# How many zero matmuls TensorE gets in each step of a two-layer transformer kernel

## The chip, the cores and the metric

The kernel runs on one core of a Trainium2 chip. A core has TensorE (matrix products, called PE in a profile), ScalarE (ACT), VectorE (DVE), GpSimd (POOL) and the queue engine SyncE (SP). The metric is the time on the device, in microseconds, of one execution: the median of several runs.

## The reference

One sequence of S = 2048 tokens with D = 640 features goes through attention block A, token mixer B, A again and B again, with the same weights both times. A has 32 heads of 20 features, B has F = 1536 hidden rows and mixes over the tokens.

```python
def _A_ref(x, wqkv, wo):
    qkv = (x @ wqkv).reshape(B, S, 3, H, Dh).transpose(2, 0, 3, 1, 4)
    q, k, v = qkv[0], qkv[1], qkv[2]
    scores = jnp.einsum("bhqd,bhkd->bhqk", q, k) * (Dh ** -0.5)
    p = _softmax(scores, axis=-1)
    o = jnp.einsum("bhqk,bhkd->bhqd", p, v)
    return o.transpose(0, 2, 1, 3).reshape(B, S, D) @ wo

def _B_ref(x, w1, b1, w2, b2):
    h = _layernorm(x, axis=-1)
    u = _gelu(jnp.einsum("bsd,sf->bdf", h, w1) + b1)
    y = jnp.einsum("bdf,fs->bds", u, w2) + b2
    return y.transpose(0, 2, 1)

x = x + _A_ref(_layernorm(x), wqkv, wo)
x = x + _B_ref(_layernorm(x), w1, b1, w2, b2)
x = x + _A_ref(_layernorm(x), wqkv, wo)
x = x + _B_ref(_layernorm(x), w1, b1, w2, b2)
```

## The kernel before

The program has five parts: the set-up with the first layer norm and the projections to V (0 to 50 us), the first attention stage (to 937 us), the first token mixer with the second layer's projections (to 1052 us), the second attention stage (to 1937 us) and the second mixer. The change lies in `attention`, which is written out twice, once for each layer.

The work of a stage is cut into units (qb, g, kt): a block of 512 queries (four of them), a group of four heads (eight) and a tile of 128 keys (16). A unit has four chunks, one for each head, of 128 keys by 512 queries. For one chunk PE makes scores S (`s_matmul`, L441) into one bank of PSUM; the exponential of them is made either by ScalarE (L474) or, for some chunks of the last key tiles, by VectorE with a polynomial (L351, L368, L374, L381, L386); PE then multiplies it by V (`emit_PV`, L683) into the accumulator `acc` of the group. Four matmuls of one PV go to four column strips of the array and start together.

Chunks are packed into score tiles `S` of three banks. `tiles[t]` is a pair: the chunks that ScalarE takes in one exponential (three, or two when the third belongs to VectorE), and the VectorE chunk or None. A step t of the loop at the end of `attention` is one such exponential; a step with fewer than three ScalarE chunks is called short. There are 683 steps in each stage. The planner counts 1.344 us for a full step and 0.92 us for a short one. There are two `S` tiles, so the scores of step t+2 wait for the exponential of step t, and only one `acc`, so the first PV of a group waits until the last group's sum has been read.

The order of the work on PE is the order in which the loop writes it, and it is kept by a chain (`pe`). In step t this is: the scores of step t+1 (`emit_S`); the PVs whose exponentials are of step t-1 or earlier; zero matmuls (`keep_busy`); side work (`emit_fills`). ScalarE's exponential of step t is written between the first two. After the 16th PV of a group `normalize` puts four VectorE instructions into that engine's queue: a transpose that reads `acc` (L486), a reciprocal, a product and a second transpose (L493).

Side work is a queue of groups of matmuls: projections of later heads to K and Q (L240, five matmuls of 512 columns), the product with `wo` (L579, L614) and the first product of the mixer (L551), each with 512-column groups and 128-column groups. A step takes 1.5 units of it if it has a PV or is short, and 3.0 otherwise, until a group ends; the step after a group's end takes none (`FILL_GAP`). `planned_fill` says ahead of a step whether it will have side work (`has_fill`). VectorE copies a finished group out of the one `misc` bank (L557, L642, and others).

A zero matmul (L464) multiplies a block of zeros by a block of ones and adds the result to a bank that is in use, which leaves it as it was. One pass is four such matmuls of 512 columns, one for each column strip. The loop before the change writes `SLOTS - 1 - n_pv - short` passes (`SLOTS` is 4, `n_pv` the number of PVs of the step) in steps without side work and with an accumulator that is in use; none where side work is planned, and none between a group's last PV and the next group's first, where `acc_tiles` is empty.

## Time and profile before

| what | value |
|---|---|
| median of 3 runs | 2018.26 us (2015.72 to 2019.93) |
| the profiled execution's own time | 2025.45 us |
| its span, first to last instruction | 2023.7 us |
| mean granted clock of TensorE | 0.975 |
| PE busy | 1723.9 us, 85% |
| ACT busy | 1801.0 us, 89% |
| DVE busy | 1388.9 us, 69% |
| POOL busy | 155.1 us, 8% |
| exponentials of ScalarE | 1366, 1709.1 us |
| zero matmuls | 5232 rows |

In the profile a row names the source line, the engine, the operation, the tile that it writes and those that it reads, their shapes, the number of such instructions, the busy time in microseconds and the mean of one in nanoseconds; behind the second bar stands the engine's idle time just before these instructions, and what ended most of it ("<-PE S L441" is a PE instruction of line 441 that writes S). A matmul's row lasts some 0.17 us longer than its columns stream, because its end is modelled; matmuls in sequence overlap, and the distance of their starts tells their cost. `PEclk` is the granted clock in tenths of full speed. In a table by stretches, each engine's busy time is followed by the number of its instructions; then come the granted clock, the share of the DMA engines and the GB/s.

### The profile page before, as it was taken

To read this page: it belongs to the slowest core of one execution; us is meant where nothing else is said; L and a number is where in the kernel's file an instruction comes from. 1 tells how busy PE (TensorE), PEld (TensorE's weight loads), DVE (VectorE), ACT (ScalarE), POOL (GpSimd) and SP (SyncE) were. 2 spreads that over 40 slices of the span, in tenths; PEclk is the share of its full clock that TensorE was granted. 3 is DMA by queue.
4 is the path that set the end of the run, shared out by engine and by line. 5 is a ranking of instruction groups with operands and counts; after the bars stand their busy time and mean duration, and the time that the engine had idled before them with its cause. 6 is when DMAs were issued, how large, how long until landed. Compare 5 with 4: busy or idle time off the path is not lost.

```text
span 2023.7 us, 39147 instructions
## 1 busy us (share of the span) xinstructions
PE 1723.9 (85%) x16395; PEld 615.5 (30%) x16592; DVE 1388.9 (69%) x2091; ACT 1801.0 (89%) x1504; POOL 155.1 (8%) x220
## 2 busy tenths in 40 slices
PE   7888888888888887887998888888888888878879
PEld 4222222232222222223542222222222222222235
DVE  6777787666766577773557787777657765767742
ACT  5999999999999999996349999999999999999952
POOL 2000000110012001110000000001000220011000
PEclk9999999999999999998999999999999999999989
DMA  6000000110134012214620000112101430233145
GB/s 135 1 1 1 1 19 26 67 49 8 34 67 68 1 40 45 42 21 136 207 83 1 1 1 1 34 33 69 38 14 40 79 56 2 59 51 43 15 149 185
DMA packets 90768, 97.34 MB, mean 48 GB/s; under 512 B 9696, under 2 KB 68192, under 8 KB 90592
## 3 DMA queue, kind: packets, MB, share of 16 engines
q1 hardware_dynamic: 70464, 71.22, 11.3%
q0 software_dynamic: 20128, 23.62, 7.8%
q8 instruction: 129, 2.11, 0.4%
q14 instruction: 47, 0.39, 0.1%
HBM read 55.48 MB, written 39.32 MB: 47 GB/s over the span
## 4 chain that ended last, share of the span: by engine, by line
ACT 34%; PE 23%; DVE 22%; issue 19%; DMA 1%; POOL 0%; SPq 0%; another core or an unknown queue 0%; ACTq 0%; DVEq 0%; POOLq 0%
ACT P L474 34%; PE S L441 6%; PE y L897 5%; DVE ew L351 4%; PE acc L683 3%; DVE et L374 3%; DVE Pd L381 3%; PE acc L464 2%; DVE ey L368 2%; DVE Pd L386 2%; PE pp L231 2%; DVE T L486 1%; PE misc L551 1%; PE misc L240 1%; DVE T L491 1%
## 5 line engine op out<-in xcount | busy, mean ns | idle before, releaser
L474 ACT ACTIVATE P<-S 128x1536 bf16<-128x1536 f32 (+1 forms) x1366 | 1709.1, 1447 | 58.5 <-PE S L441 43.9
L441 PE MATMUL S<-QTq,KT 32*128 32x512 bf16 x4096 | 574.6, 388 | 198.9 <-ACT P L474 137.9
L683 PE MATMUL acc<-P,Vaug 128*32 128x512 bf16 x3764 | 388.9, 396 | 27.3 <-DVE T L486 26.6
L351 DVE TENSOR_SCALAR ew<-S 128x512 int32<-128x512 f32 x332 | 226.1, 681 | 262.6 <-PE S L441 262.3
L441 PEld LDWEIGHTS <-KT 32*128 32x128 bf16 x4096 | 195.9, 91 | 689.0 <-issue 539.0
L464 PE MATMUL acc<-zr,zw 128*32 128x512 bf16 x5232 | 404.4, 388 | 0.0
L374 DVE SCALAR_TENSOR_TENSOR et<-ey 128x1024 f32<-128x1024 f32 x166 | 202.5, 1220 | 4.4
L386 DVE SCALAR_TENSOR_TENSOR Pd<-ew,Pd 128x1024 int16<-128x1024 int16 x166 | 201.3, 1213 | 2.4
L381 DVE SCALAR_TENSOR_TENSOR Pd<-et,ey 128x1024 bf16<-128x1024 f32 x166 | 200.6, 1208 | 1.6
L683 PEld LDWEIGHTS <-Vaug 128*32 128x32 bf16 x4096 | 108.1, 93 | 278.3 <-issue 278.1
L464 PEld LDWEIGHTS <-zw 128*32 128x32 bf16 x5232 | 128.8, 97 | 97.2 <-issue 41.0
L557 DVE COPY ustg<-misc 128x512 f32<-128x512 f32 (+1 forms) x144 | 69.4, 482 | 109.1 <-PE misc L551 89.6
L182 POOL TENSOR_TENSOR rstd<-veps,mhalf 128x1 f32<-128x1 f32 x64 | 38.9, 608 | 1168.9 <-DVE veps L177 1049.7
L562 POOL DMA_DIRECT2D uacc<-ustg x96 | 86.2, 899 | 435.0 <-DVE ustg L557 421.6
L368 DVE TENSOR_SCALAR ey<-ew 128x1024 f32<-128x1024 uint16 x166 | 114.8, 692 | 2.9
L551 PE MATMUL misc<-h2st,w1st 128*128 128x128 bf16 (+1 forms) x512 | 104.7, 300 | 6.6 <-DVE ustg L557 5.3
L897 PE MATMUL y<-uT,w2s 128*128 128x128 bf16 (+1 forms) x754 | 106.8, 298 | 3.8 <-ACT uT L840 3.1
L240 PE MATMUL misc<-hh,wq_pad 128*128 128x512 bf16 x268 | 84.9, 384 | 6.2 <-DVE KT L642 2.5
L240 PE MATMUL misc<-hh,wk_pad 128*128 128x512 bf16 x250 | 78.6, 388 | 6.9 <-DVE KT L642 5.0
L486 DVE STREAM_TRANSPOSE T<-acc 128x512 f32<-128x512 f32 x64 | 45.5, 711 | 55.5 <-PE acc L683 55.5
L579 PE MATMUL misc<-wo_pad,attnT 128*128 128x128 bf16 (+1 forms) x362 | 73.6, 303 | 2.0 <-issue 1.0
L897 PEld LDWEIGHTS <-w2s 128*128 128x128 bf16 x768 | 59.7, 98 | 49.4 <-issue 4.6
(86 smaller groups left out, 898.8 us busy)
## 6 DMA issues: line engine op xcount, KB each, us to landing
uacc<-ustg POOLq DMA_DIRECT2D x72, 256.0 KB, 4.0
w2s<-in_B_w_dram SPq DMA_DIRECT2D x16, 768.0 KB
w1st<-in_B_w_dram SPq DMA_DIRECT2D x36, 256.0 KB
x1in<-xd SPq DMA_DIRECT2D x24, 320.0 KB
ua<-uacc SPq DMA_DIRECT2D x24, 320.0 KB
xd<-x2s SPq DMA_DIRECT2D x16, 320.0 KB
xin<-xd SPq DMA_DIRECT2D x16, 320.0 KB
uacc<-ustg POOLq DMA_DIRECT2D x72, 64.0 KB, 2.8
```

Of the source, the lines that this page charges most:

```text
L240: pe(nc.tensor.matmul(t[:, :], lhsT=wpad[:, dt_, g, :], rhs=st.hT[:, dt_, tb * 512:(tb + 1) * 512], start=(dt_ == 0), stop=(dt_ == NDT - 1)))
L351: first = nc.vector.tensor_scalar(out=ve_w[p][:, slot, :], in0=St[:, 2, :], scalar1=ve_scale * 65536.0, scalar2=-127.0 * 65536.0, op0=ALU. ...
L368: nc.vector.tensor_scalar(out=y[:, 0:512 * k], in0=frac, scalar1=EXP_K / 65536.0, scalar2=EXP_K * (1.0 - EXP_ROOT), op0=ALU.mult, op1=ALU.add)
L374: nc.vector.scalar_tensor_tensor(out=box["t"][:, 0:512 * k], in0=y, scalar=EXP_P, in1=y, op0=ALU.add, op1=ALU.mult)
L381: nc.vector.scalar_tensor_tensor(out=box["P"], in0=box["t"][:, 0:512 * k], scalar=EXP_Q, in1=box["y"][:, 0:512 * k], op0=ALU.add, op1=ALU. ...
L386: nc.vector.scalar_tensor_tensor(out=bits, in0=whole, scalar=128.0, in1=bits, op0=ALU.mult, op1=ALU.add)
L441: pe(nc.tensor.matmul(St[:, slot, :], lhsT=KT[32 * j:32 * j + 32, g, kt * 128:(kt + 1) * 128], rhs=get_QT(st, qb)[32 * j:32 * j + 32, g, : ...
L464: pe(nc.tensor.matmul(acc[32 * j:32 * j + 32, :], lhsT=zw[:], rhs=zr[:].to_broadcast([128, 4, 128]), start=False, stop=False, skip_group_c ...
L474: ex = nc.scalar.activation(out=P[:, 0:ncs, :].rearrange("p a b -> p (a b)"), in_=St[:, 0:ncs, :].rearrange("p a b -> p (a b)"), func=ACT. ...
L551: pe(nc.tensor.matmul(t[:, 0:w], lhsT=states[fp]["w"][:, sti, ftl * 128:(ftl + 1) * 128], rhs=tiles4[sti][:, c0:c1], start=(sti == 0), sto ...
L683: pe(nc.tensor.matmul(acc[32 * j:32 * j + 32, :], lhsT=Vaug[:, (kt * H + hh) * VW:(kt * H + hh) * VW + 32], rhs=P[:, slot, :], start=(done ...
L897: pe(nc.tensor.matmul(y[:, 0:w], lhsT=w2s[:, ft, sl * 128:(sl + 1) * 128], rhs=uT[:, ft, c0:c1], start=(ft == 0), stop=(ft == NF - 1)))
```

## The change

`SLOTS` is gone. Each step has a number of cells of 0.213 us that PE is to stream: 0.58 of its length in the planner's count, which is 3.66 for a full step and 2.51 for a short one. From that are taken the cells of the scores of step t+1 (0.25 a chunk), of the step's PVs (one each) and of its side work (one for a 512-column matmul, 0.25 for a 128-column one); the rounded rest is the number of zero passes. They are written at three places: before the last PV of a group (with two cells held back where side work is planned), after the PVs in steps without side work, and after the side work in steps with it. Where no accumulator is in use, up to two passes go to banks of the score tile of step t+1, if that tile has no VectorE chunk. The cells that a last PV's own passes took are not subtracted again in the second place.

```diff
 CFG = dict(
-    SLOTS=4,
+    ACTIVE=0.58,
...
-            fill_state = dict(cur=None, idx=0, tile=None, cooldown=0, unit=0)
+            fill_state = dict(cur=None, idx=0, tile=None, cooldown=0, unit=0, cells=0.0)
...
-            def keep_busy(count):
-                for acc in acc_tiles.values():
-                    for _ in range(count):
-                        for j in range(4):
-                            pe(nc.tensor.matmul(acc[32 * j:32 * j + 32, :], lhsT=zw[:], rhs=zr[:].to_broadcast([128, 4, 128]), start=False,
-                                                stop=False, skip_group_check=True, tile_position=(0, 32 * j)))
+            def zero_pass(bank):
+                for j in range(4):
+                    pe(nc.tensor.matmul(bank[32 * j:32 * j + 32, :], lhsT=zw[:],
+                                        rhs=zr[:].to_broadcast([128, 4, 128]), start=False, stop=False,
+                                        skip_group_check=True, tile_position=(0, 32 * j)))
+
+            def keep_busy(count, t):
+                banks = list(acc_tiles.values())
+                if not banks and t + 1 in S_tiles and tiles[t + 1][1] is None:
+                    banks = [S_tiles[t + 1][:, i, :] for i in range(min(2, len(tiles[t + 1][0])))]
+                    count = min(count, 2)
+                for i in range(count if banks else 0):
+                    zero_pass(banks[i % len(banks)])
...
+                    fs["cells"] += 1.0 if grp["cost"][fs["idx"]] > 0.5 else 0.25
...
                 n_pv = 0
+                short = len(tiles[t][0]) < 3
+                cells = 0.25 * sum(len(x) if isinstance(x, list) else x is not None
+                                   for x in (tiles[t + 1] if t + 1 < NTILES else ()))
+                want = CFG["ACTIVE"] * (0.92 if short else 1.344) / 0.213
                 while (n := pv_next(t, n_pv)) is not None:
+                    if pv_count.get(units[n][0:2], 0) == NKT - 1:
+                        keep_busy(int(want - cells - n_pv - 1 - 2 * has_fill + 0.5), t)
                     emit_PV(n)
...
-                short = len(tiles[t][0]) < 3
+                cells += n_pv
                 if not has_fill:
-                    keep_busy(CFG["SLOTS"] - 1 - n_pv - short)
+                    keep_busy(int(want - cells + 0.5), t)
+                fill_state["cells"] = 0.0
                 emit_fills(CFG["FILL_PV"] if n_pv or short else CFG["FILL_NOPV"], misc_alloc)
+                if has_fill:
+                    keep_busy(int(want - cells - fill_state["cells"] + 0.5), t)
```

## The prediction

> **What bounds the kernel now.** I read the page first, then the busy time by stage, then the timeline of TensorE around the places where a group of heads ends, and last the same steps of the two attention stages against each other. The page:
>
> ```profile
> PE 1723.9 (85%) x16395; PEld 615.5 (30%) x16592; DVE 1388.9 (69%) x2091; ACT 1801.0 (89%) x1504; POOL 155.1 (8%) x220
> ...
> PEclk9999999999999999998999999999999999999989
> ...
> L474 ACT ACTIVATE P<-S 128x1536 bf16<-128x1536 f32 (+1 forms) x1366 | 1709.1, 1447 | 58.5 <-PE S L441 43.9
> L441 PE MATMUL S<-QTq,KT 32*128 32x512 bf16 x4096 | 574.6, 388 | 198.9 <-ACT P L474 137.9
> ...
> L464 PE MATMUL acc<-zr,zw 128*32 128x512 bf16 x5232 | 404.4, 388 | 0.0
> ```
>
> ScalarE is the engine that is full, with 1366 exponentials (L474, one per step). It idles 58.5 us before them in the whole run, 43.9 us of that for score matmuls. That is all that any change of the attention loop can win from waiting. TensorE waits 137.9 us for exponentials before score matmuls, so it has slack, but not everywhere. Busy time by stage (columns after the length: PE, weight loads, DVE, ACT, POOL, then the granted clock):
>
> ```profile
> 52.55:936.70 884.15, 752.66 (x7440) 246.57 (x7519) 625.90 (x867) 851.19 (x681) 64.50 (x84) 0.98 0.14 29
> ...
> 1052.50:1936.70 884.20, 757.37 (x7444) 245.77 (x7528) 624.32 (x861) 854.42 (x683) 64.48 (x84) 0.98 0.14 31
> ```
>
> The two attention stages are 884 us each, ACT 96 to 97% busy. The clock is 0.98, not 1: in the records of it, 17 times in these stages it goes to one half, each time for a stretch of 3.41 us or two in a row, 21 stretches in all. What one costs is seen because both stages run the same plan. Steps 52 to 63 in either:
>
> ```profile
> 114.33:130.82 16.49, 14.33 (x142) 4.02 (x136) 11.72 (x14) 14.77 (x12) 0.00 (x0) 0.90 0.00 1
> 1117.27:1132.97 15.70, 13.07 (x142) 4.19 (x136) 11.64 (x14) 14.53 (x13) 0.00 (x0) 1.00 0.01 1
> ```
>
> The first stage has the drop here (clock 0.90) and the second has not, and the same eleven steps take 0.79 us more. Five further such pairs give 0.80, 0.65, 0.84, 1.20 and 1.25, mean of the six 0.92; one pair with a drop of two stretches gives 2.50, 1.25 for each.
>
> **What precedes a drop.** I laid a grid of 3.41 us over the timeline, in phase with the drops, and added up in each window the time in which matmuls stream (512 columns 0.213 us; the four matmuls of a pass, which start together, once). The mean is 0.62. The 17 windows before the drops hold 0.26 to 0.47; of windows under 0.35 all are followed by one, of those from 0.35 to 0.43 about half, of those over 0.49 none. One of them on TensorE:
>
> ```profile
> 490.29 0.39 PE L441 MATMUL S<-QTq,KT 32*128 32x512 bf16 x3
> 492.23 0.40 PE L683 MATMUL acc<-P,Vaug 128*32 128x512 bf16 x4 [1.54 <-DVE T L486]
> 492.44 0.62 PE L464 MATMUL acc<-zr,zw 128*32 128x512 bf16 x8
> 492.99 0.82 PE L441 MATMUL S<-QTq,KT 32*128 32x512 bf16 x3
> ```
>
> The only accumulator is being transposed, the next group's first PV waits 1.54 us, and the clock halves at 493.24. A rule of the Trainium skill speaks against the change here: "TensorE: Matmul & The Clock Gate", section "HAM oscillation — how this bites in real kernels", says to avoid idle gaps over about 3.4 us. The longest gap in the 17 windows is 2.45 us, so the trace has drops without such a gap. By the rule alone fewer short gaps would be worth nothing, and the sum below would lose its gain and come to about +11 us.
>
> **The change, counted.** Zero passes alter nothing that the planner looks at, so its 1366 steps stay as they are, and old and new rule can be worked out over the same list of steps. The old rule gives 1308 passes, the 5232 rows of the page by four; the new one 1626. In the 638 steps without side work that hold an accumulator nothing moves (3, 2 or 1 passes by both, but for two steps). The 318 new passes are: 236 in 192 steps with side work (one or two where the fill is short: four 128-column matmuls, or the odd fifth of a projection), 36 in 18 steps between accumulators, 44 in 22 short steps that end a group (one before the last PV, one after), 2 others. Of all these, 74 in 50 steps go into the score tile that the next exponential reads; that is a new kind of work before a wait of ACT.
>
> **Gain of clock.** A pass adds 0.213 of 3.41 us, 0.0625, to its window. In the 17 windows the new passes that fall in them lift eight over 0.48 (five single drops, three double, so 11 stretches); nine stay at 0.26 to 0.474, four of them because they get no pass. The phase of the grid is luck, but over all phases the windows under 0.43 fall by about the same share, from 15 to 6. 11 stretches at 0.92 to 1.25 us are 10 to 14; I take 11, by the six single pairs. Ends: 0, and 21 stretches or 20 us.
>
> **Cost in the score tile.** A step that ends a group, on PE and on ACT:
>
> ```profile
> 710.39 0.39 PE L441 MATMUL S<-QTq,KT 32*128 32x512 bf16 x3
> 710.71 0.40 PE L683 MATMUL acc<-P,Vaug 128*32 128x512 bf16 x4
> 711.15 0.40 PE L441 MATMUL S<-QTq,KT 32*128 32x512 bf16 x3
> 712.50 0.39 PE L441 MATMUL S<-QTq,KT 32*128 32x512 bf16 x3 [0.95 <-ACT P L474]
> ```
>
> ```profile
> 710.89 2.90 ACT L474 ACTIVATE P<-S 128x1536 bf16<-128x1536 f32 x2
> ```
>
> The pitch of a pass is 0.217 (three passes of zeros end 0.44 later than one: 0.83 and 0.39 us in the timeline). With one pass before the PV and one after it into the tile written at 710.39, the last stream ends at 710.71 + 3 x 0.217 = 711.36. ACT starts some 0.28 after a stream ends (here 771.84 less 771.34 less 0.213; the median of 105 such starts is 0.28):
>
> ```profile
> 771.34 0.39 PE L441 MATMUL S<-QTq,KT 32*128 32x512 bf16 x3
> ...
> 771.84 1.45 ACT L474 ACTIVATE P<-S 128x1536 bf16<-128x1536 f32 x1 [0.87 <-PE S L441]
> ```
>
> So the exponential of 710.89 starts at 711.64, 0.75 late, of which 0.11 costs nothing since it was recorded as starting 0.21 before its predecessor's end where 0.10 is the least. That is 0.64 us lost. The same for all 50 steps: 24 short ones lose 13.2 us together (0.28 to 0.76 each), ten others 3.0, sixteen full steps with slack nothing: 16.2 us. Part of that is swallowed by idle time that ACT has anyway within the next ten steps, because DVE has the end of a group to normalize (transposes of 0.71 and 0.70, a product of 0.68) and PE waits for it. By the starts of the exponentials, read one by one, the sites at steps 257, 343, 428, 471, 556, 599, 641 and 663 are followed by such a loss of at least their own delay, in both stages, 8.5 us. What is left is 7.7. Ends: 0, if DVE's backlog swallows all, and 16.2.
>
> **Cost of the rest.** The 236 passes behind side work push the next score matmul by 0.22 or 0.43. Where PE would have waited for the exponential (504 waits, 137.9 us, 0.27 each) this is free, and an exponential's score tile is ready a step ahead. Carried forward step by step against the idle time before each score matmul and its lead over its exponential, 36 places are left where ACT gets it, 5.8 us together, 2.5 of it beside today's drops; I take 3. Ends: 0 and 5.8. The 22 passes ahead of a last PV could put off the transpose by 0.22 each; at 710.71 it begins only at 712.33, DVE being at another row until then, so I take 0; end 4.8. No DMA, queue of SP or POOL, or instruction of ACT or DVE is added.
>
> The sum: -11 + 7.7 + 3 = -0.3 us. The profiled execution took 2025.45 us (span 2023.7 and 1.75 around it), 7.2 above the median of the three runs, 2018.26; I put the difference on the median: 2018.0. About 0.2%, 4 us, is what a measurement can tell from no change.
>
> **The rivals.** Faster: DVE's backlog after each group swallows nearly all of the 16.2 us, since a late exponential gives DVE time, and the drops go by 11 to 15 stretches: -11 to -15, and 0 to 5 back, about 2008. For it: eight of the delayed sites per stage are followed by idle ACT. Against: at 300, 450, 492, 513 and 620 nothing follows that could take it.
>
> Slower by the score tile: the exponential's new wait for zero passes, in the steps that end a group, is not swallowed: -11 + 16.2 + 3 = +8, 2026. It decides from the point where more than 12 of the 16.2 us stay. For it: the pitch of a short step, 0.90 us, cannot hold 0.32 + 3 x 0.22 + 0.28 us. Against: the idle ACT just named.
>
> Slower since the clock is not kept: the passes go where the idle stretches are not; the waits for T and for ew stay, and as many drops come at other phases: 0 to -4, + 10.7, about 2027. For it: four of the 17 windows get no pass. Against: the windows' shares.
>
> **How the numbers follow.** No change that can be told 0.36, faster 0.31, slower by the score tile 0.22, by the clock 0.11. The likeliest reaches from 2014 to 2022. The far ends, all drops gone at no cost (1998) and none gone at full cost (0 + 16.2 + 5.8 + 4.8, 2045), need every term at its end together; a tenth on each side lies outside 2005 to 2031. Faster 0.31, same 0.36, slower 0.33.
>
> **What would show it.** Right: 6504 rows of zero matmuls, some 300 of them writing S; 6 to 13 half-clock stretches in the attention stages; ACT's idle time for PE grows at short steps that end a group by 0.3 to 0.76 us, with zero passes named as what ended it. Wrong: 17 or more stretches (then the third rival), or exponentials at those steps that start as before (then the tile's wait costs nothing and the kernel is faster), or ACT's idle time before L474 more than 10 us away from 58.5.

## The result: 0.4 to 0.6% slower

| | before | after |
|---|---|---|
| median | 2016.99 us (2014.83 to 2019.93) | 2029.52 us (2026.91 to 2030.85) |
| ratio after / before, 95% | | 1.006 [1.0042, 1.0077] |
| the same two kernels, timed again later | 2020.87 us | 2028.52 us, 1.0035 [1.0023, 1.0047] |
| profiled execution, own time / span | 2025.45 / 2023.7 us | 2030.38 / 2028.6 us |
| granted clock | 0.975 | 0.988 |
| stretches at half clock in the attention stages | 21 | 6 |
| ScalarE's idle time before the exponentials | 58.5 us | 63.9 us |
| both attention stages, first to last exponential of each, added | 1764.1 us | 1770.9 us |

The kernel is slower; "no change" was forecast. The first comparison rests on four executions of each kernel, and those of the kernel before (to 2019.9 us) lie in the lower part of what more executions later gave (2014 to 2030), so 1.0035 is the safer ratio. The time of 2029.5 lies within the range of 2005 to 2031 and next to the rival "slower by the score tile" (2026). The page of the kernel after (L481 is what L474 was, L690 was L683, L462 was L464):

```profile
PE 1785.7 (88%) x17660; PEld 627.3 (31%) x17864; DVE 1390.8 (69%) x2091; ACT 1802.5 (89%) x1504; POOL 154.3 (8%) x220
...
L481 ACT ACTIVATE P<-S 128x1536 bf16<-128x1536 f32 (+1 forms) x1366 | 1710.5, 1415 | 63.9 <-PE S L441 35.0
L441 PE MATMUL S<-QTq,KT 32*128 32x512 bf16 x4096 | 567.5, 384 | 146.6 <-ACT P L481 85.7
L462 PE MATMUL acc<-zr,zw 128*32 128x512 bf16 x6208 | 488.4, 384 | 0.5 <-issue 0.5
```

PE is 62 us busier, and no other engine's busy time changed by more than 2 us (PEld, its weight loads, by 12). PE's waits for exponentials before scores fell from 137.9 to 85.7 us: that slack was filled, as meant. The other 296 rows of zeros write S; they are seen when groups are listed by line with shapes kept apart:

```profile
L462 PE MATMUL S<-zr,zw 128*32 128x512 bf16 x296 | 24.9, 383 | 0.0
```

**The clock.** Steps 52 to 63 in both stages, the pair that the prediction used (busy time by stretch, granted clock third from the end):

```profile
114.06:129.80 15.74, 13.16 (x142) 4.30 (x136) 11.53 (x14) 14.52 (x12) 0.00 (x0) 1.00 0.01 2
1121.56:1137.30 15.74, 13.16 (x142) 4.30 (x136) 11.53 (x14) 14.52 (x12) 0.00 (x0) 1.00 0.00 1
```

The first stage took 16.49 us here at a clock of 0.90 and now takes 15.74 at 1.00, as long as its twin. 0.75 us for one stretch is inside the 0.65 to 1.25 that the prediction read.

**The new wait.** ScalarE's waits of the kernel after, by what ended them (sum in us, number, longest):

```profile
ACT P L481 <- PE S L441: 35.0, 68, 2.2
ACT P L481 <- PE S L462: 17.6, 30, 1.0
ACT P L481 <- PE acc L690: 8.9, 20, 0.9
```

The second line did not exist before: 30 exponentials wait for a pass of zeros. One of them, at step 513 of the first stage (start, length, engine, line), on PE and on ACT:

```profile
709.76 0.39 PE L441 MATMUL S<-QTq,KT 32*128 32x512 bf16 x3
710.09 0.40 PE L462 MATMUL acc<-zr,zw 128*32 128x512 bf16 x4
710.31 0.39 PE L690 MATMUL acc<-P,Vaug 128*32 128x512 bf16 x4
710.53 0.39 PE L462 MATMUL S<-zr,zw 128*32 128x512 bf16 x4
```

```profile
711.03 2.79 ACT L481 ACTIVATE P<-S 128x1536 bf16<-128x1536 f32 x2 [0.55 <-PE S L462]
```

Scores, zeros, last PV and zeros follow each other 0.22 to 0.33 apart. The last stream ends at 710.53 + 0.213 = 710.74, and the exponential starts 0.29 later, 1.27 after its own scores were started. Before, that distance was 0.50 (710.39 to 710.89). So it is 0.77 late; the prediction's working had 0.75 and then took 0.11 off.

**The account by steps.** The 1366 steps are the same in all kernels here, so the distance from one exponential's start to the next can be compared step by step. "Sites" are the 50 steps whose passes go into the score tile in the kernel after; "drops" are the steps from 2 us before a half-clock stretch to 6 us after it, in either of the two kernels; the rest is the rest. After against before: sites +24.3, drops -16.8, rest -0.7, sum +6.8 us. A second profile of both kernels gave the stages as 1763.7 and 1770.4, and for the second profile of the kernel after against the first of before sites +24.3, drops -17.1 and rest -0.9. The steps outside the attention stages took 1.9 us less, so the two profiled executions differ by 4.9 us only; the medians differ by 12.5 in the first comparison and by 7.7 in the second.

### The profile page after: what moved, and what is told of

It is laid out like the page before. It is cut to its first block, busy times and chain, and to the rows that moved or that the text cites. A ratio compares the mean times of both kernels' runs of the same rounds, so it can differ in the third digit from the quotient of the medians.

```text
span 2028.6 us, 41688 instructions
## 1 busy us (share of the span) xinstructions
PE 1785.7 (88%) x17660; PEld 627.3 (31%) x17864; DVE 1390.8 (69%) x2091; ACT 1802.5 (89%) x1504; POOL 154.3 (8%) x220
## 4 chain that ended last, share of the span: by engine, by line
ACT 29%; PE 23%; DVE 23%; issue 22%; DMA 1%; POOL 1%; SPq 0%; ACTq 0%; another core or an unknown queue 0%; POOLq 0%; DVEq 0%
ACT P L481 29%; PE S L441 6%; PE y L914 5%; DVE ew L351 4%; PE acc L690 3%; DVE Pd L381 3%; DVE et L374 3%; PE acc L462 3%; DVE Pd L386 3%; DVE ey L368 2%; PE pp L231 1%; DVE T L493 1%; PE misc L240 1%; PE misc L558 1%; DVE T L498 1%
## 5 line engine op out<-in xcount | busy, mean ns | idle before, releaser
L481 ACT ACTIVATE P<-S 128x1536 bf16<-128x1536 f32 (+1 forms) x1366 | 1710.5, 1415 | 63.9 <-PE S L441 35.0
L441 PE MATMUL S<-QTq,KT 32*128 32x512 bf16 x4096 | 567.5, 384 | 146.6 <-ACT P L481 85.7
L462 PE MATMUL acc<-zr,zw 128*32 128x512 bf16 x6208 | 488.4, 384 | 0.5 <-issue 0.5
L690 PE MATMUL acc<-P,Vaug 128*32 128x512 bf16 x3764 | 384.6, 391 | 25.2 <-DVE T L493 24.6
L441 PEld LDWEIGHTS <-KT 32*128 32x128 bf16 x4096 | 185.1, 91 | 655.0 <-issue 505.8
L462 PEld LDWEIGHTS <-zw 128*32 128x32 bf16 x6504 | 155.0, 96 | 142.0 <-issue 70.6
L690 PEld LDWEIGHTS <-Vaug 128*32 128x32 bf16 x4096 | 107.1, 93 | 267.5 <-issue 266.9
```

What stands on the lines that cost most here:

```text
L441: pe(nc.tensor.matmul(St[:, slot, :], lhsT=KT[32 * j:32 * j + 32, g, kt * 128:(kt + 1) * 128], rhs=get_QT(st, qb)[32 * j:32 * j + 32, g, : ...
L462: pe(nc.tensor.matmul(bank[32 * j:32 * j + 32, :], lhsT=zw[:], rhs=zr[:].to_broadcast([128, 4, 128]), start=False, stop=False, skip_group_ ...
L481: ex = nc.scalar.activation(out=P[:, 0:ncs, :].rearrange("p a b -> p (a b)"), in_=St[:, 0:ncs, :].rearrange("p a b -> p (a b)"), func=ACT. ...
L690: pe(nc.tensor.matmul(acc[32 * j:32 * j + 32, :], lhsT=Vaug[:, (kt * H + hh) * VW:(kt * H + hh) * VW + 32], rhs=P[:, slot, :], start=(done ...
```

## The experiments

All kernels, in the order in which they were run; the ratio is to the kernel before on the same chip. "Stretches" (at half clock, in the attention stages) and "both stages" are from one profiled execution. "Clock" is from all executions: the mean granted clock of this kernel's executions less that of the executions of before on the same chip, in thousandths. A stretch of 3.41 us at one half lowers the mean clock over 2024 us by 0.84 thousandths, so +12.7 thousandths stand for 15 stretches fewer. The standard error of these differences is 0.7 to 1.2 thousandths (1.6 for misc_bank), one to two stretches.

| kernel | zero passes | ratio, 95% | median us | clock | stretches | both stages us |
|---|---|---|---|---|---|---|
| before_again | 1308 | 0.9997 [0.9981, 1.0012] | 2021.25 | -0.1 | 23 | 1763.7 |
| no_score_tile | 1552 | 1.0003 [0.9988, 1.0017] | 2023.59 | +7.1 | 6 | 1758.4 |
| no_side | 1390 | 1.0013 [0.9998, 1.0027] | 2023.34 | +8.8 | 9 | 1762.2 |
| misc_bank | 1626 | 1.0114 [1.0091, 1.0137] | 2046.44 | +2.8 | 23 | 1795.0 |
| after_again | 1626 | 1.0035 [1.0023, 1.0047] | 2028.52 | +12.7 | 6 | 1770.4 |
| acc_instead | 1626 | 1.0032 [1.002, 1.0044] | 2027.71 | +8.3 | 8 | 1766.6 |
| side_only | 1530 | 1.005 [1.0033, 1.0067] | 2031.88 | +0.5 | 17 | 1770.1 |
| full_gaps | 1566 | 1.0055 [1.0043, 1.0067] | 2032.47 | +0.9 | 17 | 1771.3 |
| pre_only | 1330 | 0.9974 [0.9964, 0.9985] | 2016.77 | +3.6 | 16 | 1755.7 |
| pre_all | 1370 | 0.9989 [0.9975, 1.0003] | 2019.63 | +4.6 | 16 | 1761.1 |
| pre_gaps | 1366 | 0.9956 [0.9939, 0.9973] | 2013.14 | +7.5 | 11 | 1752.5 |
| no_pre | 1604 | 1.0043 [1.0026, 1.006] | 2030.7 | +8.5 | 10 | 1770.6 |
| short_only | 1330 | 1.0003 [0.9987, 1.0018] | 2020.58 | +3.5 | 13 | 1757.6 |
| gaps_only | 1344 | 1.0007 [0.9989, 1.0026] | 2021.11 | +0.6 | 19 | 1763.3 |
| pre_gaps_side | 1588 | 1.002 [1.0007, 1.0033] | 2024.83 | +7.2 | 12 | 1764.6 |
| side_narrow | 1504 | 1.0006 [0.9994, 1.0018] | 2023.73 | +5.6 | 16 | 1765.1 |
| side_wide | 1450 | 0.9987 [0.9975, 1.0] | 2017.92 | +5.2 | 14 | 1759.6 |

### First: what does each new place cost?

**before_again** is the kernel before, unchanged.

> The kernel before, unchanged, profiled a second time. Both theories expect 2017 us. What it tells apart is the drops of the clock: the first profile had 21 half-clock stretches in the attention stages and ran 2025 us, 8 us above the runs without a profile. If the phase of the clock's grid is luck, this profile has another number of them (10 to 20), at other steps, and its time goes with the number by about 1 us a stretch. If the profile itself slows the kernel, it has about 21 again and takes about 2025 us.

It measured 0.9997. The second profile has 23 stretches and took 2022.9 us, 1.6 above its median: neither 10 to 20 stretches nor 2025 us again. 12 of its 16 drops lie within two steps of a drop of the first profile, so the places are largely the kernel's, and luck decides about the rest. In this comparison the kernel before ran from 2014.2 to 2027.6 us; so a single execution of it says little, and differences of 0.2% need the intervals. Much of this spread goes with the clock: over the 116 executions of the kernel before in all comparisons (2014 to 2030 us, granted clock 0.969 to 0.982) time and clock have a correlation of -0.82, and a thousandth less of clock goes with 1.12 us more. That is 0.94 us for a stretch, an estimate that agrees with the 0.92 of the prediction's pairs of steps. It also means that a profile's count of stretches is one draw; the column "clock" is the better guide.

**no_score_tile** leaves out the 74 passes into the score tile and keeps all others.

```diff
 def keep_busy(count, t):
     banks = list(acc_tiles.values())
-    if not banks and t + 1 in S_tiles and tiles[t + 1][1] is None:
-        banks = [S_tiles[t + 1][:, i, :] for i in range(min(2, len(tiles[t + 1][0])))]
-        count = min(count, 2)
```

> The changed kernel without the zero passes that go into the next score tile (74 passes less); the passes before a group's last PV and behind side work stay. Theory 'score tile' (the exponential waits for the passes written into its tile): the 24.3 us that the exponentials at these 50 steps lost in the profile go, some drops of the clock come back (9 to 13 stretches for 6), the time falls by 12 to 20 us from the changed kernel's 2029.5, to 2010 to 2017: faster than the kernel before or equal to it. Rival 'PE time' (passes behind side work put off the score matmuls): it stays within 5 us of the changed kernel, above 2024 us.

1.0003, 2023.6 us, some 0.3% below the kernel after: more than the rival allows and less than the 12 to 20 us of the theory. The sites came to +1.8 instead of +24.3, so the lateness at the sites is due to these passes. The profile has the same 6 stretches, but it is the fastest of twelve executions: their clocks run from 0.979 to 0.987, all below the 0.988 to 0.992 of the kernel after, and the column gives 8 stretches fewer than before, where after has 15 fewer. So the passes into the score tile do hold clock: 5.6 thousandths or, by an estimate at 0.92 us a stretch, some 6 us in a typical execution, which this pair of profiles, equal in stretches, doesn't show. Step by step between these two kernels, the 74 passes cost 22.5 us at the sites, 0.5 around drops, and 10.5 of it was swallowed in the rest: 12.5 us net in the stages at an equal number of stretches. But the kernel is not faster than before, so something else costs about as much as the clock brings: the rest is +6.8 against before, 4.3 of it at steps 560, 601 and 602, which come as late or later in side_only below.

**no_side** leaves out the 236 passes of the steps with side work, and with them 16 of the 74 in the score tile.

```diff
 emit_fills(CFG["FILL_PV"] if n_pv or short else CFG["FILL_NOPV"], misc_alloc)
-if has_fill:
-    keep_busy(int(want - cells - fill_state["cells"] + 0.5), t)
```

> The changed kernel without the passes behind side work (236 less, 16 of them into a score tile). Theory 'score tile': nearly all of the loss stays, since 68 of its passes into score tiles in the steps without side work stay... by the list 58 of 74 stay and cost about 19 of the 24.3 us; with the drops that come back (10 to 15 stretches) the time is 2028 to 2036, not below the changed kernel's. Rival 'PE time': the passes behind side work were the cost, and the time falls to 2015 to 2020.

1.0013, 2023.3 us, 8.7 us less in the stages than after. Faster than the theory had it (2028 to 2036) and slower than the rival (2015 to 2020). The lateness at the sites fell to 16.6, so 7.7 of the 24.3 come from passes behind side work. Where that happens is seen at step 428, after:

```profile
600.20 0.40 PE L462 MATMUL acc<-zr,zw 128*32 128x512 bf16 x4
600.53 0.39 PE L441 MATMUL S<-QTq,KT 32*128 32x512 bf16 x3
600.86 0.40 PE L462 MATMUL acc<-zr,zw 128*32 128x512 bf16 x4
601.08 0.39 PE L690 MATMUL acc<-P,Vaug 128*32 128x512 bf16 x4
601.30 0.39 PE L462 MATMUL S<-zr,zw 128*32 128x512 bf16 x4
```

The first pass stands behind the side work of the step before and puts off the scores by one pitch and a change of tile; then the two passes around the PV come on top. The exponential is 0.85 late here, 0.52 without the passes behind side work; at step 257 1.09 and 0.77, at 599 1.01 and 0.52. At steps 343, 471, 492 and 513, which no side work precedes, the two kernels agree within 0.02.

**misc_bank** puts the 74 passes into the bank of the side work, which no exponential reads.

```diff
-if not banks and t + 1 in S_tiles and tiles[t + 1][1] is None:
-    banks = [S_tiles[t + 1][:, i, :] for i in range(min(2, len(tiles[t + 1][0])))]
-    count = min(count, 2)
+if not banks and count > 0 and t + 1 in S_tiles and tiles[t + 1][1] is None:
+    fresh = fill_state["cur"] is None
+    bank = misc_alloc() if fresh else fill_state["tile"]
+    for i in range(min(count, 2)):
+        zero_pass(bank, fresh and i == 0)
+    return
```

> The changed kernel with the same number of passes in the same places of TensorE's order, but those of the steps without an accumulator go to the bank of the side work, which no exponential reads. It leaves PE's time as it is and takes away the wait. Theory 'score tile': ACT's wait for zero passes is gone, the clock keeps its 4 to 9 half-clock stretches, and the time falls by 12 to 20 us, to 2010 to 2017. Rival 'PE time': PE is as late as in the changed kernel and so are the exponentials: 2025 to 2032. A third outcome is a new wait, of the passes for VectorE's copy of that bank, which would show as PE idle ahead of the zero passes and give back a part.

1.0114, 2046 us: neither of the two theories, but the new wait that was named as a third outcome, and it gives back more than a part. The passes wait for VectorE to copy the last finished group out of the only `misc` bank, and PE, which goes in order, waits with them. Their row, by shapes (idle time before them and what ended it behind the second bar):

```profile
L462 PE MATMUL misc<-zr,zw 128*32 128x512 bf16 x296 | 26.3, 402 | 25.8 <-DVE ustg L567 10.9 <-DVE QTq L652 6.7 <-DVE x1s L599 4.1
```

The exponentials no longer wait at the sites (+1.7), but the rest of the steps lost 22.8 us, and the half-clock stretches are 23. This bank is worse than the score tile.

### Second: where did the rest of the gain go?

**after_again** is the kernel after, unchanged, beside the next three.

> The changed kernel, unchanged, timed beside the kernel before on this chip, so that the variants below are compared on one chip. 1.004 to 1.0075 of the kernel before; 4 to 9 half-clock stretches in the attention stages; the order of VectorE's instructions is the changed kernel's, word for word.

1.0035, with the same 6 stretches, the same 24.3 us at the sites and the same order of VectorE's instructions. The loss is real, and nearer to 0.4% than to 0.6%.

**acc_instead** takes the pass that would follow a group's last PV and puts it ahead of that PV, into the accumulator.

```diff
 while (n := pv_next(t, n_pv)) is not None:
     if pv_count.get(units[n][0:2], 0) == NKT - 1:
-        keep_busy(int(want - cells - n_pv - 1 - 2 * has_fill + 0.5), t)
+        ended = not has_fill
+        open_ = ended and t + 1 in S_tiles and tiles[t + 1][1] is None
+        late = min(2, max(0, int(want - cells - n_pv - 1 + 0.5))) if open_ else 0
+        keep_busy(int(want - cells - n_pv - 1 - 2 * has_fill + 0.5) + late, t)
 ...
-if not has_fill:
+if not has_fill and not ended:
     keep_busy(int(want - cells + 0.5), t)
```

> The changed kernel with all 1626 passes, but in the 22 short steps that end a group the pass that went into the score tile goes into the accumulator, before the last PV, beside the one that is there already. TensorE has the same work in the same step; the exponential has no pass to wait for. Theory 'score tile': the 18.6 us that the exponentials lost at the 24 short steps fall to under 3, the time falls by 7 to 12 us from the changed kernel's, to about that of the kernel before (0.998 to 1.003). Rival 'PE time': the step is as full as before, its scores as late, and the time stays within 3 us of the changed kernel. A third thing can go against it: the accumulator's transpose comes one pass later still (0.22 us), which may cost VectorE's order again.

1.0032: the expectation failed. 7 to 12 us less than the kernel after was expected, and the medians differ by 0.8, which is the rival's number, though not for its reason. The lateness at the 24 short sites did go, from 18.6 to 2.6 us, but the stages are only 4.4 us shorter than after's: 13.1 gained at the sites, 5.4 lost in the rest, where part of this lateness had been swallowed, and 3.3 around drops (8 stretches instead of 6). By the clock of all executions (+8.3 for +12.7) it has 5 stretches more than the kernel after, which takes back the rest of the gain.

**side_only** has only the passes of steps with side work (no passes in the score tile, none ahead of a last PV).

```diff
 def keep_busy(count, t):
     banks = list(acc_tiles.values())
-    if not banks and t + 1 in S_tiles and tiles[t + 1][1] is None:
-        ...
 ...
-    if pv_count.get(units[n][0:2], 0) == NKT - 1:
-        keep_busy(int(want - cells - n_pv - 1 - 2 * has_fill + 0.5), t)
```

> Only the passes behind side work: none into a score tile, none ahead of a last PV (1530 passes). In the variant without score tile passes the exponentials lost 1.16 us at step 560 and 1.00 at 601 and 602, in both stages, where VectorE's queue has the transpose of the accumulator behind a step of the polynomial instead of ahead of it. Theory 'order': that swap comes from the pass ahead of the last PV; without it the transpose stands ahead again at these two places, 4.3 us come back, and the time is 0.996 to 0.999 of the kernel before, with 6 to 12 half-clock stretches. Rival 'side passes': the lateness is that of the passes behind side work in the steps before (555, 598); the two places lose as much as there, and the time stays at 0.999 to 1.002.

1.0050, above both expectations: slower than before on its own, with 17 stretches still there and a clock like before's (+0.5). The lateness at steps 560, 601 and 602 stayed, so it doesn't take a pass ahead of the last PV. ScalarE's idle time in it:

```profile
L478 ACT ACTIVATE P<-S 128x1536 bf16<-128x1536 f32 (+1 forms) x1366 | 1709.3, 1432 | 64.2 <-PE S L441 49.0
```

Before it was 58.5, 43.9 of that for scores. The passes behind side work make the scores late, and alone they buy hardly any clock.

**full_gaps** is side_only with the 36 passes of full steps between accumulators (`if not banks and gap and ...`, with `gap` true where `not short and n_pv == 0`).

> The passes behind side work, and two passes into the score tile in the 18 full steps without PV and side work, where TensorE had slack for them (1566 passes); none in short steps, none ahead of a last PV. Theory 'score tile': the wait costs only where the step is too short for it, so these 36 passes cost under 1.5 us in all (the 18 steps lost 0.4 us at 237 and 0.6 at 365 in the changed kernel, nothing at most others), the clock keeps 4 to 9 half-clock stretches, and the time is 0.995 to 0.999 of the kernel before, not above side passes alone. Rival 'any pass into the score tile costs': it is over 1.001.

1.0055, again missed, and for the same reason; the number is the rival's, but side_only has it without these passes: the 36 made no difference to it. What remained by now as the source of the gain were the 22 passes ahead of a last PV, which the prediction had counted in the clock and else at nothing.

### Third: the passes ahead of the last PV

**pre_only** is the kernel before with these 22 passes alone.

```diff
+short = len(tiles[t][0]) < 3
 while (n := pv_next(t, n_pv)) is not None:
+    if pv_count.get(units[n][0:2], 0) == NKT - 1 and n_pv == 0 and short and not has_fill:
+        keep_busy(1)
     emit_PV(n)
```

> The kernel before with one thing of the change: the one zero pass ahead of a group's last PV in the 22 short steps without side work (1330 passes). Side passes alone kept 17 half-clock stretches in their profile, side passes and these 22 together 6. Theory 'the pass at the group's end holds the clock': about 8 to 14 stretches for 21 before, VectorE's order nearly that of the kernel before, and 5 to 11 us less: 0.9945 to 0.9975 of the kernel before. Rival 'chance of the grid': the 6 and the 17 were luck of the clock's phase; it has 16 to 23 stretches and a time of 0.998 to 1.002.

0.9974, as expected: 22 passes, 4.8 us of work for PE, make the kernel 5 us faster. The stretches were not as expected: 16, at the rival's lower end, where the theory had 8 to 14. That it isn't chance of the grid is seen from the clock of all twelve executions: +3.6 thousandths, 4 stretches, some 4 us. By steps, the whole -8.4 us of the profile stands around drops (16 stretches against 21), and sites and rest are 0.0; that of the rest is a balance, since the exponential after step 560 comes 1.24 us later in the first stage.

**pre_all** writes such a pass ahead of each of the 62 last PVs in the loop (the condition without `n_pv == 0 and short and not has_fill`).

> The same ahead of the last PV of every one of the 64 groups, also in steps with side work (some 1370 passes). Theory 'group's end': a few drops fewer than with 22 such passes, 0 to 3 us faster than that variant. Rival 'VectorE's order': in steps with side work the pass shifts the order of VectorE's queue, and the exponentials after the 40 other group ends come later: 2 to 8 us slower than with the 22 alone.

0.9989, with the same 16 stretches as pre_only and the same gain around drops (-8.8), but +5.4 us in the rest. The 40 passes more buy little clock (+4.6 for +3.6) and cost 0.13 us each, within the rival's number. Its cause isn't shown: the order of VectorE differs from before in 44 places, against 40 in pre_only.

**pre_gaps** adds to pre_only the 36 passes between accumulators in full steps.

```diff
-def keep_busy(count):
-    for acc in acc_tiles.values():
+def keep_busy(count, gap=False, t=0):
+    banks = list(acc_tiles.values())
+    if not banks and gap and t + 1 in S_tiles and tiles[t + 1][1] is None:
+        banks, count = [S_tiles[t + 1][:, 0, :]], 2
+    for acc in banks:
 ...
-    keep_busy(CFG["SLOTS"] - 1 - n_pv - short)
+    keep_busy(CFG["SLOTS"] - 1 - n_pv - short, not short and n_pv == 0, t)
```

> The 22 passes ahead of last PVs, and two passes into the next score tile in the 18 full steps without PV and side work; no side passes, none in short steps (1366 passes). Theory 'score tile costs only in short steps': 5 to 10 stretches, no exponential waits more than 0.4 us for the 36 passes, 0.993 to 0.997 of the kernel before and not slower than the 22 passes alone. Rival 'any pass into the score tile costs': slower than those by 5 us or more.

0.9956 [0.9939, 0.9973], 2013.1 us: this beats both kernels, with 58 of the 318 new passes; the 11 stretches are one more than expected. Its page, and its list of ScalarE's waits:

```profile
PE 1755.6 (87%) x16824; PEld 616.2 (31%) x16824; DVE 1389.9 (69%) x2091; ACT 1800.0 (90%) x1504; POOL 155.3 (8%) x220
...
L477 ACT ACTIVATE P<-S 128x1536 bf16<-128x1536 f32 (+1 forms) x1366 | 1707.9, 1437 | 48.0 <-PE S L441 35.0
```

```profile
ACT P L477 <- PE S L441: 35.0, 64, 2.1
ACT P L477 <- PE acc L686: 9.7, 18, 1.6
```

Passes into the score tile of a full step are there (144 rows), but the list has no wait for them: the sites cost 1.9 us together. ScalarE idles 48.0 us before exponentials, 10.5 less than before.

### Fourth: one place at a time

**no_pre** is the kernel after without the 22 passes ahead of a last PV.

> The changed kernel without the 22 passes ahead of last PVs (1604). Theory 'group's end': the exponentials at the short group ends start 0.22 us earlier each (24.3 us of loss at the 50 steps become 19 to 20), but the clock drops more often, 9 to 15 stretches for 6, so that the time stays within 4 us of the changed kernel. Rival 'the pass in the short step is pure cost': no more stretches than 7, and 4 to 6 us faster than the changed kernel.

1.0043, 1770.6 us in the stages, as after, and as expected. So the passes that are worth 8.4 us in pre_only are worth nothing on balance here, but not because the clock has no use for them: without them there are 10 stretches instead of 6 (and the clock of all executions is +8.5 instead of +12.7), which loses 4.9 us around drops, while the sites gain 4.7, 0.22 for each pass.

**short_only** is the kernel before with just those: one pass into the score tile behind the last PV of a short step (`short and n_pv == 1`).

> The kernel before with the disputed 22 passes alone: one into the next score tile in each short step that ends a group without side work (1330 passes); nothing before a last PV, nothing behind side work. Theory 'score tile in short steps': the exponentials after these steps start some 0.45 to 0.75 us late, 10 to 16 us over the 22; the clock drops a little less often (14 to 20 stretches); 1.002 to 1.006 of the kernel before. Rival 'they cost only together with the pass before the PV, which makes the step too long': under 4 us of such lateness, 0.998 to 1.001.

1.0003, where a loss was expected. The lateness is there, 10.2 us at the sites, but 8 stretches fewer in this profile give 11.8 back and the rest another 4.9. By the clock of all executions both kinds of pass do much the same (+3.5 and +3.6, 4 stretches); the one ahead of the PV does it with no lateness at the sites, the one behind for 10 us. With both, the second kind doesn't pay: from pre_gaps to no_side, which differ in these 22 passes (and in 2 others and a choice of bank), the time goes from 0.9956 to 1.0013, and the stages are 9.7 us longer (+14.7 at the sites, -0.8 around drops, -4.2 in the rest).

**gaps_only** is the kernel before with the 36 passes of full steps.

> The kernel before with the 36 passes into score tiles in full steps without PV and side work, and nothing else (1344 passes). Theory: these passes are free and hold the clock through the wait for the accumulator: 12 to 17 stretches, lateness at these steps under 2.5 us in all, 0.996 to 0.999 of the kernel before. Rival 'the gain of 22 + 36 passes came from the 22 alone': 0.999 to 1.001.

1.0007, no difference: 1.8 us at the sites, 19 stretches. Alone they buy no clock (+0.6). Beside the passes ahead of the PV they help: +7.5 for +3.6, and 0.9974 to 0.9956; these two intervals overlap, but on the same chip the medians are 2016.8 us of twelve executions (from 2014.5) and 2013.1 of six, five of which lie under 2014.

**pre_gaps_side** is pre_gaps with the passes behind side work.

> The changed kernel without its passes into score tiles in short steps and in steps with side work; those in full steps, the ones before a last PV and those behind side work stay (1588 passes). If the parts add up, it is the 0.9956 of passes before last PVs and in full gaps plus the price of the passes behind side work (0.3 to 0.5 per cent by two pairs of variants): 0.998 to 1.001. Rival 'the passes behind side work cost only what the idle clock leaves': with the clock held by the others it is 0.994 to 0.997.

1.002, just above what was expected, 0.64% above pre_gaps, and 12 stretches against 11. They bought no clock here (+7.2 for +7.5).

### Fifth: why do passes behind side work cost so much?

**side_narrow** and **side_wide** are pre_gaps_side with the passes only behind 128-column side work (138) or only behind 512-column side work (84).

```diff
 fs["cells"] += 1.0 if grp["cost"][fs["idx"]] > 0.5 else 0.25
+fs["narrow"] = grp["cost"][fs["idx"]] <= 0.5
 ...
-if has_fill:
+if has_fill and fill_state.get("narrow"):      # side_wide: and not fill_state.get("narrow")
```

> Passes before last PVs and in full gaps as in the variant at 0.9956, and behind side work only where it is of 128-column matmuls (138 of the 220 passes there). These fills are short, so the pass comes where TensorE has time in its own step, but VectorE copies the side work's bank next and the group's other half follows. If the price of side passes sits here: 0.998 to 1.002. If not: 0.995 to 0.997.

> The same with the passes only behind side work of 512-column matmuls (82 passes: the odd fifth of a projection, two matmuls of the mixer's product in a step without PV). If the price of side passes sits here: 0.998 to 1.002, with exponentials late after these steps. If not: 0.995 to 0.997. If both halves are within 0.001 of half the price, it is spread over all of them and no single kind of step is the cause.

1.0006 and 0.9987: both lose against pre_gaps, 0.50 and 0.31%, or 12.6 and 7.1 us in the stages; with both it was 0.64% and 12.1. Of the 12.6, 6.7 lie around drops (16 stretches against 11), 4.1 in the rest and 1.8 at the sites; of the 7.1, 4.5, 2.6 and 0.1. One way in which it happens is seen at the end of a group at steps 599 to 602. PE and then DVE in pre_gaps:

```profile
816.56 0.39 PE L441 MATMUL S<-QTq,KT 32*128 32x512 bf16 x3
...
817.11 0.39 PE L686 MATMUL acc<-P,Vaug 128*32 128x512 bf16 x4
817.48 0.39 PE L441 MATMUL S<-QTq,KT 32*128 32x512 bf16 x3
818.46 0.40 PE L686 MATMUL acc<-P,Vaug 128*32 128x512 bf16 x4 [0.59 <-DVE T L489]
```

```profile
817.09 0.68 DVE L368 TENSOR_SCALAR ey<-ew 128x1024 f32<-128x1024 uint16 x1
817.69 0.71 DVE L489 STREAM_TRANSPOSE T<-acc 128x512 f32<-128x512 f32 x1
818.33 1.18 DVE L374 SCALAR_TENSOR_TENSOR et<-ey 128x1024 f32<-128x1024 f32 x1
```

And in side_narrow:

```profile
820.92 0.62 PE L462 MATMUL acc<-zr,zw 128*32 128x512 bf16 x8
821.47 0.39 PE L441 MATMUL S<-QTq,KT 32*128 32x512 bf16 x3
...
822.02 0.39 PE L690 MATMUL acc<-P,Vaug 128*32 128x512 bf16 x4
822.34 0.39 PE L441 MATMUL S<-QTq,KT 32*128 32x512 bf16 x3
824.12 0.40 PE L690 MATMUL acc<-P,Vaug 128*32 128x512 bf16 x4 [1.40 <-DVE T L493]
```

```profile
822.22 1.23 DVE L374 SCALAR_TENSOR_TENSOR et<-ey 128x1024 f32<-128x1024 f32 x1
823.36 0.71 DVE L493 STREAM_TRANSPOSE T<-acc 128x512 f32<-128x512 f32 x1
```

Two passes behind side work push the scores and the group's last PV back. In pre_gaps the transpose T starts 0.58 after that PV, ahead of the product et; in side_narrow et goes first, T starts 1.34 after the PV, and the next group's first PV waits 1.40 instead of 0.59. The exponential of step 602 then comes 0.73 later after its predecessor than in pre_gaps. No half-clock stretch follows here; that a longer wait like this one empties a window and brings a drop elsewhere is not shown.

This is one place. How much of the 3 to 12 us is owed to the order of VectorE, how much to the clock and how much to plain lateness is not settled: the order of VectorE differs from the kernel before in 40 places in pre_only and pre_gaps, which are faster, and in 88 in side_only, which is slower. The clock can't be the whole of it: pre_gaps_side is 0.64% slower than pre_gaps at nearly the same clock.

## Why the prediction was wrong

The profiled stages, taken apart in one order, with the ratios beside them:

| from, to | passes added | both stages | ratio |
|---|---|---|---|
| before, pre_gaps | 22 ahead of last PVs, 36 between accumulators | -11.6 us | 1 to 0.9956 |
| pre_gaps, no_side | 22 in short steps' score tiles, 2 others | +9.7 | to 1.0013 |
| no_side, after | 236 in steps with side work | +8.7 | to 1.0035 (first comparison: 1.006) |

- **What bounds the kernel, and the count:** right. 6504 rows of zeros, 296 of them into S, and the same 1366 exponentials.
- **Gain of clock (-11):** right in mechanism, on the small side. 15 stretches went instead of 11, and the steps around drops are 16.8 to 17.1 us shorter; 6 are left, the lower end of "6 to 13". The clock of all executions gives 15 stretches too. By the shares over a window of 3.41 us at any phase, the windows under 0.43 fell to about four tenths, as forecast (15 to 6). The Trainium skill, "TensorE: Matmul & The Clock Gate", section "HAM oscillation — how this bites in real kernels", warns of idle gaps above about 3.4 us; the drops here came without such a gap and went when gaps that were shorter were filled, so for this kernel the share of the window was the better guide.
- **Score tile (16.2 gross, 8.5 swallowed, 7.7 net):** this is the first step that failed, by its size. Gross 22.5 us (after against no_score_tile), 10.5 swallowed, 12.5 net at an equal number of stretches (in the time of all executions, with the clock that these passes hold, 0.3%, some 6 us). The swallowing was read rightly: it is seen behind seven of the eight sites named, all but 257. The 24 short steps lost 18.6 us instead of 13.2. Two terms were wrong. The 0.11 us that the forecast took off each lateness "since it was recorded as starting 0.21 before its predecessor's end" was not granted: step 513 was worked out as 0.75 and lost 0.77, but went into the sum as 0.64. Without the passes behind side work the 24 steps lose 14.75, which is about this correction. Of the other 3.9 us, 1.2 are at step 641, where the pass into the tile itself stands behind side work, and 2.7 are an interaction: where the step before has side work, its new pass makes the same scores later still (step 599: 0.52 and 1.01). The forecast priced the two kinds of pass apart. The full steps with slack were right: 18 of them cost 1.5 us.
- **Side work (3; ends 0 and 5.8):** the second step that failed, and above its upper end. Without these passes the stages are 8.7 us shorter (7.8 of it at the sites: the 3.9 at short steps just told, and as much at steps of the score tile's kind that have side work themselves). Over five pairs of kernels with and without them it is 2.7 to 12.1 us in the stages, 0.2 to 0.6% in the time. The forecast carried lateness forward along PE and ScalarE only, and left VectorE's order as it was. It also put part of the clock's gain down to these passes, which alone bring hardly any (side_only +0.5) and none on top of pre_gaps (+7.2, +5.6 and +5.2 for +7.5), though the kernel after has +12.7 and no_side, without them, +8.8. Lateness at the sites is 7.8 of the 8.7 us here; what makes their price in the other pairs stays open.
- **Passes ahead of a last PV (0; end 4.8):** nothing lost by them alone, as said, at 22 places where the transpose waits for another row anyway. But the clock's gain was put down to all new passes alike, and these 22 alone bring half of it in the profiles (pre_only has -8.4 us) and 3.6 of 12.7 thousandths in the clock of all executions. In pairs with and without them the stages change by -8.4, -10.8, -6.7 and -11.7 us, and by 0.3 where the short steps' passes are there too.
- **The sum:** -0.3 was forecast. With the measured terms it would be -16.8 + 12.5 + 8.7 = 4.4; the stages show +6.8, since the terms come from different pairs of kernels and overlap, and the two profiled executions +4.9. The medians rose by more, 7.7 and 12.5: the profiled execution of before lay 8.5 us above the median of the first comparison and that of after 0.9 above its own. The prediction put such a distance on both alike, which was wrong by 7.6 us in the first comparison; a second profile of both lay 1.6 and 2.1 above the medians. The profiled execution of before, at a clock of 0.975, lies on the slow side of the spread told under before_again.
- **The rivals:** "slower by the score tile" was to give +8 us and comes nearest, by its own condition too, if barely: more than 12 us stayed, 12.5. Its "against", idle ScalarE behind the sites, was as large as said (10.5 for 8.5); the gross was larger. It doesn't explain the loss alone: no_score_tile, with the score tile left out, is no faster than before, since it also loses clock against the kernel after (+7.1 for +12.7) and keeps the cost of the side work's passes. "Faster" needed nearly all swallowed. "The clock isn't kept" is excluded by 6 stretches and by the clock of all executions.
- **The signs named ahead:** those under "right" came true, but for 8 of the 24 short steps whose lateness was above 0.76 us (0.85 to 1.10 at steps 257, 428, 556 and 599 of both stages), and ScalarE's idle time, 63.9, stayed within 10 us of 58.5, though the kernel is slower. That last sign could not tell the cases apart: it nets the new waits (17.6 us for passes of zeros) against shorter waits for scores (43.9 to 35.0).

## What to carry to other kernels

Filler for the clock is worth something only in the windows that fall short, so find those and put single passes there, in a place from which the full engine does not wait: 22 passes ahead of a last PV brought -0.26%, 318 everywhere +0.4 to 0.6%. Filling to an even share puts most passes where the clock was safe, and every pass between side work and the next scores, or in a tile that another engine is about to read, can come out as lateness. When several small changes touch the same step, price them together: a pass that costs nothing alone can come out as lateness beside another. And a single profile's count of half-clock stretches is one draw: take the clock over all executions before calling a place useless.

## What the runs showed of the hardware that was not expected

- Half-clock stretches do not need a long gap. In the kernel before, 17 drops followed windows with shares of 0.26 to 0.47 and no gap above 2.45 us; in the kernel after, five drops are left, behind windows of 0.24 to 0.39.
- An exponential starts 0.29 us after the last zero stream into its tile (711.03 for 710.74), as it does after a score: an addition of zeros to the tile is waited for like any other write.
- The time of one and the same kernel goes with how often its clock is halved: over 116 executions of the kernel before, 1.12 us for each thousandth of the mean granted clock, with clocks of 0.969 to 0.982.
- The order in which VectorE works differs from the kernel before though no VectorE instruction was touched: in no place for before_again and gaps_only, in 8 for short_only, 40 for pre_only, 100 for after. Two profiles of one kernel agree in every place (before and before_again, after and after_again), so the order goes with the program and not with the execution. What decides it was not tried; a change of PE's work alone can thus move work on another engine.
